# Retention, a mixture of experts and a dense layer on one core: float32 scores without splits, expert rows gathered tile by tile, gates applied to the dense result

## The chip, the core and the metric

The kernel runs on one core of a Trainium2 chip. The core has five engines that work from queues of their own: PE (TensorE, matrix products; PEld is its loading of the stationary operand), DVE (VectorE), ACT (ScalarE), POOL (GpSimd) and SP (SyncE, which here only starts DMAs). POOL also starts the indirect DMAs, which fetch or send rows by a list of row numbers. [...] The metric is the time of one execution on the device in microseconds (us): 1457.0 as the median of three runs (1452.89, 1457.00, 1457.19).

## The reference

Three stages follow each other, in float32 (the dense weights come as float64):

```python
# retention: B, H, S, D = 8, 8, 576, 64
scores = scale * np.matmul(q, k.transpose(0, 1, 3, 2))
ret = scores * np.where(rel >= 0, gamma[:, None, None] ** rel, 0.0)
x = np.matmul(ret, v)                                   # -> 4608 tokens of 512 features
# experts: 8 of them, 512 -> 1024 -> 512, the best one for each token
logits = x @ w_gate
expert_idx = np.argmax(logits, axis=1)
probs = softmax(logits)                                 # sum + 1e-09
gate_w = probs[np.arange(N), expert_idx]
out[mask] = gate_w[mask, None] * (np.maximum(x[mask] @ w1[e], 0.0) @ w2[e])
# dense: 512 -> 2048 -> 512
r = np.maximum(out @ w_in, 0.0)
result = (r * r) @ w_out
```

## The kernel before

The 4608 tokens are 36 tiles of 128. The order of the instructions on each engine is the order in which the code is written (a manual schedule); the framework puts in the semaphores. Pools with a fixed number of buffers decide when a transfer may start.

**Retention** (the loop `for t in range(NT)`, lines 592 to 635). SP loads one tile's q, k and v four tiles ahead (`load(t + 4)`, line 595) into a pool of five buffers. For each tile PE makes the scores of the next tile (`scores(t + 1)`, line 613), every second tile the router's logits (line 417), then the output `out_x(t)` (lines 385 and 389) and the running state `state(t)` (line 361). DVE multiplies the scores by a mask (line 343), scales the output (line 397) and transposes it (line 399); SP writes it to DRAM as `x_d`. ACT copies the state (line 368). POOL scales v (line 316). After some tiles DVE also does the routing of a group of tiles, one step for each turn of the loop.

Two ways to make the scores are in the code. The first `EASY = 2` tiles multiply k and q in plain float32: for each of four pairs of heads two products, one on partitions 0 to 63 and one on 64 to 127 (line 330). All later tiles first go through `split(t + 3)` (lines 293 to 312): k and q are rounded to float32r (ACT, lines 299 and 302), the remainders are taken (DVE and POOL, lines 303 and 306), and q is laid into `qb`, whose other half is zero, so that one product of 128 rows and 256 columns covers two heads. Three such products (high by high, high by low, low by high: lines 338 to 340) make one score.

**Experts** (lines 649 to 947). Work goes by units: `u = 8 * e + f` is one eighth of expert `e`. A unit's first product (`first`, lines 746 to 748) is made one unit ahead of its second (`second`, lines 770 to 772); both are split in float32r, three products each. Each expert has 640 slots for tokens, five tiles. `gather(e + 1)` fetches all five tiles at the start of expert `e`: 20 indirect DMAs on POOL, in one go, into a pool `xs_p` of one buffer. Five more fetch the logits of those tokens (`fetch_logits`, one unit later). `transp` transposes and splits one tile in each of the units `f = 2` to `6` (DVE line 718, ACT line 722, DVE line 723). `gate_of` makes the gates, and `finish` scales the result by them and sends the rows to `y_d`. At unit `REST = 18` a branch (line 793) skips the work for tokens beyond the slots; here it is skipped.

**Dense layer** (lines 950 to 1046): nine blocks of 512 tokens, two products (line 971, and lines 992 to 994), the square between them, and `store`, which copies the result out of PSUM.

Of the kernel before, what the change touches and what calls it, by code (L numbers as in the profile page):

```python
# [27 lines left out]
EASY = 2  # L28
BUSY = 6
# [10 lines left out]
def body(ctx, tc, att, tab_v, tab_x, masks, wg, ident, pick, cst, wu, wd, out):  # L40
# [19 lines left out]
    l_d = dram.tile([NTOK, NE], F32, name="l_d")  # L60
# [3 lines left out]
    cf = const.tile([128, C_N], F32, name="cf")  # L64
    ub = places.tile([128, 128], BF16, name="ub")
# [45 lines left out]
    # ---- float64 weights: sign, exponent and 20 bits of the mantissa come from the high word, the  # L111
    # other 32 bits from the low word; kept in DRAM as two float32r parts ----
# [99 lines left out]
    def fetch_logits(sm, index, n):  # L212
        lg = sm.tile([128, n, NE], F32, tag="lg", name="glg")
        for i in range(n):
            fetch_rows(lg[:, i], l_d[:, :], index[:, i:i + 1])
        return lg
# [18 lines left out]
    def gate_of(sm, lg, n):  # L235
        mx = sm.tile([128, n], F32, tag="mx", name="gmx")
        vec.tensor_reduce(out=mx, in_=lg, axis=AX.X, op=ALU.max)
        vec.tensor_tensor(out=lg, in0=lg, in1=mx.unsqueeze(2).to_broadcast([128, n, NE]), op=ALU.subtract)
        act.activation(out=lg, in_=lg, func=AF.Exp)
        vec.tensor_reduce(out=mx, in_=lg, axis=AX.X, op=ALU.add)  # L240
        vec.tensor_scalar(out=mx, in0=mx, scalar1=1e-9, scalar2=None, op0=ALU.add)
        g = sm.tile([128, n], F32, tag="g", name="gg")
        vec.reciprocal(out=g, in_=mx)
        return g
# [3 lines left out]
    # ================= retention, logits and routing =================  # L248
# [5 lines left out]
    with ExitStack() as es:  # L254
# [17 lines left out]
        qb = [[tabs.tile([128, 4, 2, 128], F32R, name=f"qb{i}{s}") for s in range(2)] for i in range(3)]  # L272

        in_t, vs_t, k_t, r_t, st_acc, xp_t = {}, {}, {}, {}, {}, {}
# [18 lines left out]
        def split(t):  # L293
            q = in_t[t][:, 0].rearrange("p (h n) -> p h n", h=4)
            k = in_t[t][:, 1]
            qh, ql = qb[t % 3]
            kh = sp_p.tile([128, 512], F32R, tag="kh", name="kh")
            kl = sp_p.tile([128, 512], F32R, tag="kl", name="kl")
            act.activation(out=kh, in_=k, func=AF.Copy)
            for s in range(2):  # L300
                o = slice(64 * s, 64 * s + 64)
                act.activation(out=qh[o, :, s], in_=q[o], func=AF.Copy)
            (pool if t > EASY else vec).tensor_tensor(out=kl, in0=k, in1=kh.bitcast(F32), op=ALU.subtract)
            for s in range(2):
                o = slice(64 * s, 64 * s + 64)
                (pool if s and t > BUSY else vec).tensor_tensor(
                    out=ql[o, :, s], in0=q[o], in1=qh[o, :, s].bitcast(F32), op=ALU.subtract
                )
            k_t[t] = kh, kl
# [12 lines left out]
        def scores(t):  # L322
            m = msk[:, 1 if kind(t)[1] == 4 else 0]
            sc = [sc_ps.tile([128, 4, 128], F32, tag="sc", name="sc") for _ in range(2)]
            for p in range(4):
                cs = slice(128 * p, 128 * p + 128)
                if t < EASY:
                    for s in range(2):
                        o = slice(64 * s, 64 * s + 64)
                        pe.matmul(  # L330
                            sc[s][:, p], in_t[t][o, 1, cs], in_t[t][o, 0, cs],
                            start=True, stop=True, skip_group_check=True,
                        )
                    continue
                qh, ql = [a[:, p].rearrange("p s n -> p (s n)") for a in qb[t % 3]]
                kh, kl = [a[:, cs] for a in k_t[t]]
                o = sc[p // 2][:, 2 * (p % 2):2 * (p % 2) + 2].rearrange("p s n -> p (s n)")
# [251 lines left out]
        if EASY < 3:  # L589
            split(2)  # L590
        fold = None
        for t in range(NT):
# [29 lines left out]
            if BUSY < t < NT - 3:  # L622
                split(t + 3)
# [501 lines left out]
```

## Time and profile before

| what | us |
|---|---|
| median of three runs | 1457.0 |
| span of the profiled execution, first to last instruction | 1541.4 |
| of it retention, to the last transpose of a tile | about 203 |
| of it experts | about 205 to 766 |
| of it the dense layer | about 766 to 1541 |

What lies around the span is not shown by the page. Over the whole span PE is busy 94%, DVE 50%, ACT 32%, POOL 26%; the 16 DMA engines moved 172.51 MB. These are means over three stages with different limits, so the rows below are taken stage by stage. [...] A table by lines gives instructions that share line, operation and shape: their busy time, the mean of one in ns, and the engine's idle time before them with what ended it.

### The profile page before, as it was taken

To read this page: it belongs to the slowest core of one execution; us is meant where nothing else is said; L and a number is where in the kernel's file an instruction comes from. 1 tells how busy PE (TensorE), PEld (TensorE's weight loads), DVE (VectorE), ACT (ScalarE), POOL (GpSimd) and SP (SyncE) were. 2 spreads that over 40 slices of the span, in tenths; PEclk is the share of its full clock that TensorE was granted. 3 is DMA by queue.
4 is the path that set the end of the run, shared out by engine and by line. 5 is a ranking of instruction groups with operands and counts; after the bars stand their busy time and mean duration, and the time that the engine had idled before them with its cause. 6 is when DMAs were issued, how large, how long until landed. Compare 5 with 4: busy or idle time off the path is not lost.

```text
span 1541.4 us, 20420 instructions
## 1 busy us (share of the span) xinstructions
PE 1445.4 (94%) x8081; PEld 1229.0 (80%) x8081; DVE 769.3 (50%) x1231; ACT 496.3 (32%) x866; POOL 397.0 (26%) x347
## 2 busy tenths in 40 slices
PE   7989899886979798789999999999999999999998
PEld 6878788685968687679888888888888888888887
DVE  7898965584848486574333333323232333323222
ACT  4555524242424243233222222222222222222222
POOL 5877736726354454711100000000000000000000
PEclk9999999988989899889999999999999999999999
DMA  8887634654546364634560202020200202020000
GB/s 308 277 265 251 206 115 141 217 166 150 187 142 218 117 223 144 197 110 183 162 252 5 51 0 55 1 55 1 55 1 1 55 1 55 1 55 0 28 0 28
DMA packets 92407, 172.51 MB, mean 112 GB/s; under 512 B 16654, under 2 KB 54030, under 8 KB 86672
## 3 DMA queue, kind: packets, MB, share of 16 engines
q1 hardware_dynamic: 82944, 151.03, 31.1%
q0 software_dynamic: 9360, 20.10, 4.1%
q8 instruction: 65, 1.06, 0.3%
q14 instruction: 38, 0.31, 0.1%
HBM read 125.86 MB, written 46.28 MB: 112 GB/s over the span
## 4 chain that ended last, share of the span: by engine, by line
PE 59%; issue 4%; DMA 1%; DVE 1%; POOL 0%; SPq 0%; ACT 0%; POOLq 0%; DVEq 0%
PE fl L971 25%; PE fa L994 8%; PE fa L993 8%; PE fa L992 8%; PE l L746 2%; PE l L747 2%; PE l L748 2%; PE acc L772 1%; PE acc L771 1%; PE acc L770 1%; DMA w<-wd_d 1%; DMA y_d<-y,sidx 0%; POOL y_d L229 0%; SPq L667 0%; DVE w L100 0%
## 5 line engine op out<-in xcount | busy, mean ns | idle before, releaser
L971 PE MATMUL fl<-xt,w 128*128 128x512 f32 (+1 forms) x1776 | 416.9, 384 | 1.8 <-DMA w<-wd_d 1.8
L971 PEld LDWEIGHTS fl<-xt,w 128*128 128x128 f32 x1776 | 328.1, 189 | 68.2 <-issue 2.2
L978 DVE TENSOR_TENSOR fr<-fr 128x512 f32<-128x512 f32 x144 | 99.9, 694 | 402.9 <-ACT fr L976 402.9
L992 PE MATMUL fa<-w,gh 128*128 128x512 f32 x576 | 224.1, 389 | 0.0
L993 PE MATMUL fa<-w,gh 128*128 128x512 f32 x576 | 224.1, 389 | 0.0
L994 PE MATMUL fa<-w,gl 128*128 128x512 f32 x576 | 224.1, 389 | 0.0
L976 ACT ACTIVATE fr<-fl 128x512 f32<-128x512 f32 x144 | 86.2, 599 | 417.6 <-PE fl L971 417.6
L746 PE MATMUL l<-xt,w 128*128 128x320 f32 (+1 forms) x480 | 154.9, 323 | 35.5 <-issue 17.5
L748 PE MATMUL l<-xt,w 128*128 128x320 f32 (+1 forms) x480 | 154.2, 321 | 11.0 <-issue 10.7
L747 PE MATMUL l<-xt,w 128*128 128x320 f32 (+1 forms) x480 | 154.5, 322 | 8.5 <-issue 8.4
L208 POOL DMA_INDIRECT xs<-x_d,qidx x140 | 151.0, 1078 | 44.3 <-issue 42.4
L982 DVE TENSOR_TENSOR gl<-fr,gh 128x512 fp32r<-128x512 f32 x144 | 99.7, 692 | 100.5 <-ACT gh L980 100.5
L772 PE MATMUL acc<-w,hl 128*128 128x512 f32 x320 | 127.4, 398 | 4.1 <-issue 3.7
L771 PE MATMUL acc<-w,hh 128*128 128x512 f32 x320 | 128.7, 402 | 2.3 <-issue 1.9
L770 PE MATMUL acc<-w,hh 128*128 128x512 f32 x320 | 128.9, 403 | 1.8 <-issue 1.8
L746 PEld LDWEIGHTS l<-xt,w 128*128 128x128 f32 x480 | 93.7, 195 | 45.3 <-issue 38.9
L980 ACT ACTIVATE gh<-fr 128x512 fp32r<-128x512 f32 x144 | 91.0, 632 | 109.8 <-DVE fr L978 109.8
L993 PEld LDWEIGHTS fa<-w,gh 128*128 128x128 f32 x576 | 108.2, 188 | 22.5
L992 PEld LDWEIGHTS fa<-w,gh 128*128 128x128 f32 x576 | 108.1, 188 | 22.5
L994 PEld LDWEIGHTS fa<-w,gl 128*128 128x128 f32 x576 | 108.0, 188 | 22.3
L753 DVE SCALAR_TENSOR_TENSOR hl<-l,hh 128x320 fp32r<-128x320 f32 (+2 forms) x128 | 59.9, 486 | 118.9 <-ACT hh L752 60.3
L747 PEld LDWEIGHTS l<-xt,w 128*128 128x128 f32 x480 | 94.0, 196 | 13.9 <-issue 11.4
(154 smaller groups left out, 1895.5 us busy)
## 6 DMA issues: line engine op xcount, KB each, us to landing
raw<-wu SPq DMA_DIRECT2D x62, 512.0 KB
in<-att SPq DMA_DIRECT2D x28, 1024.0 KB
craw<-wd SPq DMA_DIRECT2D x32, 512.0 KB
wd_d<-cw SPq DMA_DIRECT2D x32, 512.0 KB
w<-wd_d SPq DMA_DIRECT2D x16, 1024.0 KB
x_d<-xr SPq DMA_DIRECT2D x144, 64.0 KB
yi<-y_d SPq DMA_DIRECT2D x32, 256.0 KB
out<-fo SPq DMA_DIRECT2D x32, 256.0 KB
```

Source lines behind the costliest of these rows:

```text
L208: pool.indirect_dma_start(out=xs, out_offset=None, in_=src, in_offset=bass.IndirectOffsetOnAxis(ap=index, axis=0),)
L746: pe.matmul(ps, w[:, 0, k], hi[:, k, cs], start=(k == 0), stop=False)
L747: pe.matmul(ps, w[:, 0, k], lo[:, k, cs], start=False, stop=False)
L748: pe.matmul(ps, w[:, 1, k], hi[:, k, cs], start=False, stop=(k == 3))
L770: pe.matmul(acc[i], hh[:, cs], w[:, 0], start=(f == 0), stop=False)
L771: pe.matmul(acc[i], hh[:, cs], w[:, 1], start=False, stop=False)
L772: pe.matmul(acc[i], hl[:, cs], w[:, 0], start=False, stop=(f == 7))
L971: pe.matmul(ps, w[:, s, k], x[:, k, ts], start=(n == 0), stop=(n == 11))
L978: vec.tensor_tensor(out=gg, in0=r, in1=r, op=ALU.mult)
L992: pe.matmul(acc[i], gh[:, cs], w[:, 0], start=(f == 0), stop=False)
L993: pe.matmul(acc[i], gh[:, cs], w[:, 1], start=False, stop=False)
L994: pe.matmul(acc[i], gl[:, cs], w[:, 0], start=False, stop=(f == 15))
```

## The change

It has three parts. The constants `EASY` and `BUSY` go, and with them the tile pools' `qb` and the function `split`.

1. All tiles make the scores in plain float32, as the first two did. What is left of `split` is `spread_q`, two ACT copies for every ninth tile, now written ahead of `out_x(t)`. The zeroing of `qb` on POOL goes. The four weight splits that fall into the retention loop move from DVE to POOL.
2. `gather(e, i)` fetches one tile. Expert 1's five tiles are fetched in the units 0 to 4; those of expert `e + 2` in the units `f = 3` to `7` of expert `e`, each right behind the transpose that frees its place. The gathered rows have one buffer for good.
3. The gates leave the experts. Since relu and the square follow, a gate g on a row of the dense layer's input is g squared on the row of its result. `gates` makes the squares of all tokens in one go from the logits in SBUF; `store` multiplies by them. The table of logits in DRAM, its writes, the 40 fetches and `gate_of` go.

```diff
-        def split(t):
-            ...
+        def spread_q(t):
             if kind(t)[1] == 4:
+                q = in_t[t][:, 0].rearrange("p (h n) -> p h n", h=4)
                 act.activation(out=zq[:, :, 0], in_=q[:, :, 0:64], func=AF.Copy)
                 act.activation(out=zq[:, :, 2], in_=q[:, :, 64:128], func=AF.Copy)
...
         def scores(t):
             for p in range(4):
                 cs = slice(128 * p, 128 * p + 128)
-                if t < EASY:
-                    ...
-                pe.matmul(o, kh, qh, start=True, stop=False, skip_group_check=True)
-                pe.matmul(o, kh, ql, start=False, stop=False, skip_group_check=True)
-                pe.matmul(o, kl, qh, start=False, stop=True, skip_group_check=True)
+                for s in range(2):
+                    o = slice(64 * s, 64 * s + 64)
+                    pe.matmul(
+                        sc[s][:, p], in_t[t][o, 1, cs], in_t[t][o, 0, cs],
+                        start=True, stop=True, skip_group_check=True,
+                    )
...
-            if BUSY < t < NT - 3:
-                split(t + 3)
+            if t + 3 < NT:
+                spread_q(t + 3)
             out_x(t)
             state(t)
-            if t <= BUSY:
-                split(t + 3)
             if t % 6 == 2 and 12 <= t < 36:
-                w_q[t // 6 - 2] = split_unit(t // 6 - 2, raw.pop(t - 2), vec)
+                w_q[t // 6 - 2] = split_unit(t // 6 - 2, raw.pop(t - 2), pool)
...
+        def gates(lg):
+            e = rt.tile([128, NT, NE], F32, tag="ge", name="ge")
+            m = rt.tile([128, NT], F32, tag="gm", name="gm")
+            vec.tensor_reduce(out=m, in_=lg, axis=AX.X, op=ALU.max)
+            vec.tensor_tensor(out=e, in0=lg, in1=m.unsqueeze(2).to_broadcast([128, NT, NE]), op=ALU.subtract)
+            act.activation(out=e, in_=e, func=AF.Exp)
+            vec.tensor_reduce(out=m, in_=e, axis=AX.X, op=ALU.add)
+            vec.tensor_scalar(out=m, in0=m, scalar1=1e-9, scalar2=None, op0=ALU.add)
+            vec.reciprocal(out=m, in_=m)
+            vec.tensor_tensor(out=gate2, in0=m, in1=m, op=ALU.mult)
...
         first(4, (0,))
+        gates(lgt)
...
-            if e + 1 < NE:
-                if f == 0:
-                    gather(e + 1)
-                if f == 1:
-                    lg_t[e + 1] = fetch_logits(sm, gidx[:, CT * (e + 1):CT * (e + 2)], CT)
+            if u < CT:
+                gather(1, u)
             if e + 1 < NE and 2 <= f < 7:
                 transp(e + 1, f - 2)
+            if e + 2 < NE and f >= 3:
+                gather(e + 2, f - 3)
...
         def finish(e, tiles=range(CT)):
-                    vec.tensor_scalar(out=y, in0=acc[i], scalar1=g[:, i:i + 1], scalar2=None, op0=ALU.mult)
+                    vec.tensor_copy(y, acc[i])
...
         def store(b, tiles=range(4)):
-                    vec.tensor_copy(o, acc[i])
+                    vec.tensor_scalar(out=o, in0=acc[i], scalar1=g2, scalar2=None, op0=ALU.mult)
```

How the instructions stand now is seen best on PE, DVE and POOL. First PE in the retention loop, from the scores of tile 4 to the state of tile 3, before:

```order
L338 MATMUL sc<-qb_148,kh 128x256
L339 MATMUL sc<-qb_149,kh 128x256
L340 MATMUL sc<-qb_148,kl 128x256
...
L417 MATMUL lg<-x,wg_139 32x256 x4
L385 MATMUL x<-in,sts_142 128x128 x4
L389 MATMUL x<-r_362,vs 64x128 x4
L389 MATMUL x<-r_364,vs 64x128 x4
L361 MATMUL stp<-vs,in 64x64 x8
```

The same place of PE's queue in the changed kernel:

```order
L306 MATMUL sc<-in 128x128 x8
L386 MATMUL lg<-x,wg_139 32x256 x4
L354 MATMUL x<-in,sts_142 128x128 x4
L358 MATMUL x<-r_312,vs 64x128
L358 MATMUL x<-r_314,vs 64x128
...
L330 MATMUL stp<-vs,in 64x64 x8
```

Twelve products that read split copies (`qb`, `kh`, `kl`) have become eight that read the loaded tile `in`. DVE in one turn of the same loop, with a fold of the logits (`lgt`), before:

```order
L343 TENSOR_TENSOR r_624<-sc,msk 128x512
L343 TENSOR_TENSOR r_626<-sc,msk 128x512
L427 TENSOR_REDUCE lgt<-lg 128x16
L397 TENSOR_TENSOR x<-x,tabx 128x4x128
L399 STREAM_TRANSPOSE xr<-x 128x4x4x32
L306 TENSOR_TENSOR qb_147<-in,qb_146 64x4x128
```

The same turn on DVE now:

```order
L312 TENSOR_TENSOR r_526<-sc,msk 128x512
L312 TENSOR_TENSOR r_528<-sc,msk 128x512
L396 TENSOR_REDUCE lgt<-lg 128x16
L366 TENSOR_TENSOR x<-x,tabx 128x4x128
L368 STREAM_TRANSPOSE xr<-x 128x4x4x32
```

The remainder of q (`qb`) has gone, and nothing has taken its place. POOL from the end of the routing on, through expert 0 into expert 1 (`xs` are gathered rows, `glg` gathered logits, `w` a weight split, `y_d` the rows sent), before:

```order
L208 DMA xs<-x_d,gidx 128x512 x3
L108 TENSOR_TENSOR w<-half,w 128x512
L208 DMA glg<-l_d,gidx 128x8 x5
L208 DMA xs<-x_d,qidx 128x128 x20
L208 DMA glg<-l_d,gidx 128x8 x5
L100 TENSOR_TENSOR w<-raw,w 128x1024
L229 DMA y_d<-y,sidx 4608x512 x5
L208 DMA xs<-x_d,qidx 128x128 x20
```

The same stretch of POOL's queue now:

```order
L206 DMA xs<-x_d,gidx 128x512 x3
L106 TENSOR_TENSOR w<-half,w 128x512
L206 DMA xs<-x_d,qidx 128x128 x32
L98 TENSOR_TENSOR w<-raw,w 128x1024
L206 DMA xs<-x_d,qidx 128x128 x8
L221 DMA y_d<-y,sidx 4608x512 x5
L206 DMA xs<-x_d,qidx 128x128 x12
L98 TENSOR_TENSOR w<-raw,w 128x1024
```

The fetches of logits are gone. The 32 fetches that now stand in one row are those of expert 1 and the first three tiles of expert 2, interleaved: 16 for expert 1's tiles 0 to 3, four for expert 2's tile 0, four for expert 1's tile 4, eight for expert 2's tiles 1 and 2.

## Rows read from the trace of the kernel before

**Rows 1.** Stretches: us; PE, PEld, DVE, ACT, POOL busy (instructions); clock; DMA share; GB/s.

```profile
8.90:10.20 1.30, 1.27 (x20) 1.15 (x22) 0.00 (x0) 0.00 (x0) 0.00 (x0) 1.00 1.00 356
20.00:200.00 180.00, 160.74 (x1916) 141.79 (x1915) 163.23 (x265) 94.90 (x189) 128.79 (x96) 0.95 0.79 246
...
766.00:1541.00 775.00, 769.60 (x3387) 636.40 (x3386) 247.52 (x363) 201.36 (x330) 0.00 (x0) 1.00 0.13 37
10.00:20.00 10.00, 6.53 (x56) 5.95 (x56) 7.23 (x9) 4.31 (x8) 5.00 (x4) 0.73 1.05 414
60.00:180.00 120.00, 104.56 (x1258) 92.60 (x1255) 111.85 (x183) 64.16 (x127) 93.28 (x69) 0.94 0.83 261
...
203.00:226.00 23.00, 22.56 (x164) 19.79 (x163) 12.89 (x42) 7.54 (x16) 9.02 (x9) 1.00 0.47 139
```

**Rows 2.** Lines by shape, 20 to 200 us: busy us, mean ns, idle before.

```profile
L306 POOL TENSOR_TENSOR qb<-in,qb 64x512 fp32r<-64x512 f32 x29 | 45.2, 1557 | 3.0 <-PE turn L224 0.8
L343 DVE TENSOR_TENSOR r<-sc,msk 128x512 f32<-128x512 f32 x68 | 43.2, 675 | 0.1
L303 POOL TENSOR_TENSOR kl<-in,kh 128x512 fp32r<-128x512 f32 x32 | 43.0, 1345 | 32.4 <-ACT kh L299 32.4
...
L306 DVE TENSOR_TENSOR qb<-in,qb 64x512 fp32r<-64x512 f32 x36 | 39.6, 1101 | 12.2 <-ACT qb L302 12.1
...
L100 DVE TENSOR_TENSOR w<-raw,w 128x1024 fp32r<-128x1024 f32 x4 | 5.9, 1478 | 0.0
...
L451 DVE TENSOR_TENSOR eq<-lgt,mx 128x64 f32<-128x64 f32 x3 | 2.6, 860 | 0.1
```

**Rows 3.** Timeline, tile 1: start us, us, instruction; plain scores, then tile 0's output.

```profile
8.93 1.16 PE L330 MATMUL sc<-in 64*128 64x128 f32 x16 [2.64 <-DMA in<-att]
...
10.02 1.09 PE L389 MATMUL x<-r,vs 128*64 128x128 f32 x16
```

**Rows 4.** Timeline: first and last split scores of one tile; tile 22, load to scores.

```profile
104.09 0.60 SPq L291 DMA_DIRECT2D in<-att  x1
...
104.80 0.39 PE L338 MATMUL sc<-qb,kh 128*128 128x256 f32 x1
...
106.20 0.28 PE L340 MATMUL sc<-qb,kl 128*128 128x256 f32 x1
...
111.68 0.63 ACT L299 ACTIVATE kh<-in 128x512 fp32r<-128x512 f32 x1 [0.85 <-DMA in<-att]
...
118.29 0.39 PE L338 MATMUL sc<-qb,kh 128*128 128x256 f32 x1
```

**Rows 5.** Waits, 20 to 200 us: us in total, times, longest.

```profile
ACT kh L299 <- DMA in<-att: 30.6, 17, 3.5
```

**Rows 6.** Users of the loaded tile: ns min/median/max, first to last start us.

```profile
L299 ACT ACTIVATE kh<-in x34: 622/631/633, 12.0 to 181.7; 128x512 fp32r<-128x512 f32 x34
...
L306 DVE TENSOR_TENSOR qb<-in,qb x39: 642/1331/1579, 13.3 to 184.3; 64x512 fp32r<-64x512 f32 x39
```

**Rows 7.** Stretches in the experts; columns as in rows 1.

```profile
279.00:673.00 394.00, 331.86 (x1676) 287.71 (x1676) 248.35 (x403) 134.06 (x229) 196.02 (x179) 0.90 0.52 167
385.00:420.00 35.00, 35.00 (x199) 31.95 (x198) 29.47 (x51) 16.67 (x30) 9.39 (x8) 1.00 0.56 184
```

**Rows 8.** Waits of PE, 279 to 673 us; the first of several such rows.

```profile
PE l L746 <- issue: 17.3, 18, 1.9
```

**Rows 9.** Timelines by engine: gathering for expert 1, its last tile, PE's first unit.

```profile
226.57 1.89 POOL L208 DMA_INDIRECT xs<-x_d,qidx  x1 [1.91 <-DVE qidx L729]
...
254.56 0.95 POOL L208 DMA_INDIRECT xs<-x_d,qidx  x1 [0.31 <-issue]
...
258.63 0.71 DVE L718 STREAM_TRANSPOSE xf<-xs 128x512 f32<-128x512 f32 x1 [2.38 <-DMA xs<-x_d,qidx]
260.04 0.69 DVE L723 TENSOR_TENSOR xt<-xf,xt 128x512 fp32r<-128x512 f32 x1 [0.70 <-ACT xt L722]
...
261.99 0.31 PE L746 MATMUL l<-xt,w 128*128 128x320 f32 x1
```

More of the change, by code (lines that the diff above doesn't have):

```diff
@@ L64, in body @@
     cf = const.tile([128, C_N], F32, name="cf")
+    gate2 = const.tile([128, NT], F32, name="gate2")
     ub = places.tile([128, 128], BF16, name="ub")
@@ L210, in fetch_rows @@
         )
[L212 to L216, printed above, removed]
     x_q = x_d.rearrange("n (a c) -> (n a) c", a=4)
@@ L271, in body @@
         sts = [tabs.tile([128, 4, 128], F32, name=f"sts{i}") for i in range(4)]
-        qb = [[tabs.tile([128, 4, 2, 128], F32R, name=f"qb{i}{s}") for s in range(2)] for i in range(3)]
-        in_t, vs_t, k_t, r_t, st_acc, xp_t = {}, {}, {}, {}, {}, {}
+        in_t, vs_t, r_t, st_acc, xp_t = {}, {}, {}, {}, {}
         lead_s = []
@@ L291, in load @@
                 sp.dma_start(out=a[:, 0:n], in_=att[t, :, 0:n])
-        def split(t):
[L294 to L309, printed above, removed]
+        def spread_q(t):
             if kind(t)[1] == 4:
+                q = in_t[t][:, 0].rearrange("p (h n) -> p h n", h=4)
                 act.activation(out=zq[:, :, 0], in_=q[:, :, 0:64], func=AF.Copy)
@@ L442, in one @@
                 lg = lgt[:, t0:t1]
-                late.append(
-                    lambda: sp.dma_start(
-                        out=l_d[128 * t0:128 * t1, :].rearrange("(t p) e -> p t e", p=128), in_=lg
-                    )
-                )
                 mx = rt.tile([128, n], F32, tag="mx", name="mx")
@@ L581, in body @@
         vec.memset(wg2, 0.0)
-        for i in (0, 1, 2):
-            for a in qb[i]:
-                pool.memset(a[0:64, :, 1].bitcast(F32), 0.0)
-                pool.memset(a[64:128, :, 0].bitcast(F32), 0.0)
         scale_v(0)
@@ L588, in body @@
         scale_v(1)
-        if EASY < 3:
-            split(2)
         fold = None
@@ L695, in body, with gather @@
         acc_a = scope(es, "acc_a", 1, PSUM, reuse="tile")
-        xs_t, xt_t, lg_t, h_t, acc, gate = {}, {}, {}, {}, {}, {}
-        def gather(e):
-            xt_t[e] = columns()
-            xs = xs_p.tile([128, CT, 4, 128], F32, tag="xs", name="xs")
-            for i in range(0 if e else LEAD, CT):
-                j = CT * e + i
-                if e == 0:
-                    fetch_rows(xs[:, i].rearrange("p q c -> p (q c)"), x_d[:, :], gidx[:, j:j + 1])
-                    continue
-                for q in range(4):
-                    fetch_rows(xs[:, i, q], x_q, qidx[:, q, j:j + 1])
-            xs_t[e] = xs
+        xt_t, h_t, acc = {}, {}, {}
+        xs = xs_p.tile([128, CT, 4, 128], F32, tag="xs", name="xs")
+        def gather(e, i):
+            j = CT * e + i
+            if e == 0:
+                fetch_rows(xs[:, i].rearrange("p q c -> p (q c)"), x_d[:, :], gidx[:, j:j + 1])
+                return
+            for q in range(4):
+                fetch_rows(xs[:, i, q], x_q, qidx[:, q, j:j + 1])
         def transp(e, i):
-            xs = xs_t[e]
+            if e not in xt_t:
+                xt_t[e] = columns()
             hi, lo = [a[:, :, 128 * i:128 * i + 128] for a in xt_t[e]]
@@ L774, in finish @@
         def finish(e, tiles=range(CT)):
-            g = gate[e]
             for i in tiles:
@@ L861, in body @@
         indices(rt, NS, inv, gidx, sidx, gidf)
-        gather(0)
+        for i in range(LEAD, CT):
+            gather(0, i)
         for f in ends:
@@ L882, in body @@
         y_p = scope(es, "y_p", 5, reuse="tile")
-        sm = scope(es, "sm", 2, reuse="tile")
         lp = scope(es, "lp", 1, reuse="tile")
@@ L894, in body @@
         second(5, tiles)
-        lg_t[0] = fetch_logits(sm, gidx[:, 0:CT], CT)
         first(0, (1,))
```

40 lines of the change are left out of this document (8 added, 32 removed).

## The prediction

> **What bounds the kernel now.** I read the stretches first, then lines, waits and timelines inside the stretch that matters.
>
> The dense layer is PE alone: 769.6 of 775 us busy at a granted clock of 1.00 [rows 1]. Nothing that the change does there is on PE.
>
> In the experts PE also sets the pace, where nothing disturbs it: 199 products in 35.0 us [rows 7]. At that pace the 1676 products from 279 to 673 us would take 1676 / 199 x 35.0 = 294.8 us. They took 394: 99.2 us are lost. PE stands there without a semaphore to wait for ("issue") [rows 8], and its mean clock was 0.90 [rows 7]. Now the profiled span is 1541.4 us and the median of the timed runs 1457.0, 84.4 less, and neither of the other two stages shows a loss of that size. So I take it that the timed runs hold at most 99.2 - 84.4 = 14.8 us of it, less if some time lies around the span. [...] So every term below is taken off the median; the span of a profiled execution of the new kernel may differ from its timed runs by another amount.
>
> Retention is where several limits stand close together. From 20 to 200 us there are 34 tiles (two rows of line 343 each), 5.29 us a tile [rows 1, 2]. DVE is busy 163.2 of 180 us, PE 160.7, POOL 128.8, the DMA engines 0.79. No engine is full, and yet ACT waits 30.6 us for loads [rows 5]. The reason is a ring. Tile 22's load is issued at 104.09, its data are there at 111.68 (7.6 us), and its scores start at 118.29, after 6.6 us of splitting on ACT, DVE and POOL [rows 4]. Then the tile keeps its buffer through its scores, its output one turn later and its state: some two turns. With five buffers a turn P must satisfy 5 P >= 7.6 + 6.6 + 2 P, so P >= 4.7 us, before any jitter. That and DVE's 4.8 us a tile (163.2 / 34) make the 5.29.
>
> **The change, part by part.**
>
> PE's scores. Twelve split products start every (106.20 - 104.80) / 11 = 0.127 us, 1.53 us a tile [rows 4]. Eight plain ones (16 records, since each is recorded twice) run from 8.93 to the next product at 10.02: 1.09 us, at a clock of 1.00 [rows 1, 3]. The pairs on the two halves of the partitions overlap in this. So PE saves 0.44 us a tile, 15 us in 34 tiles, and its 160.7 us become 145.7, 4.29 a tile.
>
> [...] In the row the output of the other shape starts at 10.02, before the modelled end of the scores at 10.09 [rows 3], so no gap is seen. [...]
>
> DVE, POOL, ACT. DVE loses 39.6 us of remainders and the four weight splits, 5.9 us [rows 2]: 163.2 - 45.5 = 117.7, 3.46 a tile. It stops being a limit. POOL loses 45.2 + 43.0 = 88.2 us and gains four splits; one is twice as large as a remainder of 1.345 us [rows 2], so an estimate of 2.7 each, 11 in all. POOL goes from 128.8 to some 52 us. DVE's remainders took 642 ns at best and 1579 at worst [rows 6], so DVE is held up while POOL works; less of that remains, and I count it as nothing, because DVE now has a third of its time to spare. ACT loses all roundings. Its two copies for every ninth tile now stand ahead of the state's copies and wait for a load that was issued two turns before; at 7.6 us a load against two turns of 4.6 that costs nothing, and 3 us four times if it comes late.
>
> The ring. Without the 6.6 us it needs 5 P >= 7.6 + 2 P, P >= 2.5. It is no limit any more, and SP can issue a load as soon as a state is done.
>
> What is late next. PE needs 145.7 us for the 34 tiles, the DMA engines 0.79 x 180 = 142 us at a share of 1. The best case is that PE waits for nothing: 180 - 146 = 34 us gained. The worst is that PE keeps all of its present idle time, 19.3 us: 15 us gained. I take 24, a stretch of 156 us, nearer to the middle since the wait that the ring made goes and the one for the DMA engines comes: they would be busy 142 / 156 = 0.91. That can be had: 1.05 stands from 10 to 20 us, at 414 GB/s, with loads in large pieces [rows 1]. A share of 0.83 over two thirds of the stage, at a pace that the ring held back, is the row against more.
>
> The tail. The last tile's data are there at 181.7 us [rows 6]. Its 6.6 us of splitting lie behind that. Between 0 and 6.6 us go; I take half, 3.
>
> The gates. Six operations on DVE and one on ACT come in between routing and experts, none longer, by its row, than the 0.86 us of a similar subtraction [rows 2]: 0 to 5.2 us on DVE. Queued behind them are the transposed rows and the remainders for expert 0. PE is busy 22.56 of 23 us there [rows 1], so a delay of DVE can show; but DVE itself is busy 12.89 of 23. I take 1.5. What goes for it (fetches of logits, the gates of each expert) lay beside PE's work, and the multiplies in `finish` and `store` are passes over the same data on the same engines with or without a gate; PE covers them all but the last one. Together nothing.
>
> The gathers. POOL took from 226.57 to 255.51 for 20 fetches, 1.45 us each [rows 9]. It starts when the row numbers are there, so it can start no sooner. Expert 1's last tile was fetches 17 to 20 and is now 21 to 24, because four for expert 2 are written ahead: 4 x 1.45 = 5.8 us later. Before, its transpose began at 258.63 and its remainder was done at 260.73; PE's second half of the first unit, which reads it, began at 261.99, so there were 1.3 us to spare. Now PE waits 5.8 - 1.3 = 4.5 us, and behind the waiting transpose on DVE stand the remainder of the unit before and a weight split. It can be 0, if the fetches go faster, and 8, if the clock falls during the wait. I take +4.5. From expert 2 on each tile is fetched five units or more ahead, so those waits go; of the 14.8 us that the timed runs may have lost in the experts I count none in the forecast.
>
> Sum: 1457.0 - 24 - 3 + 1.5 + 4.5 = 1436.0 us. The forecast's own range is 1424 (retention 34) to 1448 (retention 15 and the higher costs).
>
> **The rivals.**
>
> A. The DMA engines are the limit already. If they get no better share than the 0.83 of the middle of the stage [rows 1], the stretch takes 142 / 0.83 = 171 us, 9 gained, no tail gained, and the gates and gathers eat most: 1457 - 9 + 6 = 1454. For it: the share is near 1 where loads run undisturbed. Against it: loads waited for buffers, not buffers for loads.
>
> B. The loss in the experts is in the timed runs after all. It came while POOL issued 25 fetches in a row; spread over units of 7 us they leave room. Then up to 14.8 us more go: 1421. Were the profile longer for a reason that the trace does not show, it could be the whole 99 us, 1337. For it: the loss repeats with the fetches. Against it: the 84.4 us.
>
> C. Slower than before: the clock. TensorE's clock was granted at 0.73 from 10 to 20 us, where PE was busy 65%, and at 0.95 where it was busy 89% [rows 1]. [...] Each tile has 4.29 us of PE work at full speed and as much again at half. The net gain of 21 us is gone when one seventh of the tiles (21 / (34 x 4.29) = 0.14) run at the lower level beyond today's share; at half of them the time is 1436 + 73 = 1509. Against it: by the sum PE is busier than before, 93% of 156 us, and the two plain tiles ran at 1.00.
>
> **How the numbers follow.** Forecast 0.67, A 0.12, B 0.15 (0.03 of it for the far end), C 0.06. The time is the forecast's, 1436. The range, 1416 to 1450, holds the forecast but for its upper edge, the near end of B and a part of A. About 0.3% (4.4 us) is what a measurement of this kernel can tell from no change, so "same" is 1452.6 to 1461.4: most of A, a little of the forecast and of C, 0.10. Faster: 0.65 + 0.15 + 0.05 = 0.85. Slower: 0.05, nearly all C.
>
> **What would show it.** Right, if the profile after has retention some 25 us shorter, DVE busy about two thirds of it, the DMA share near 0.9, and loads that land well before their scores. The scores' step is wrong if the 16 records of a tile take over 1.4 us; the ring's if loads still land just before they are used; the gathers' if the transpose of expert 1's last tile keeps its distance to PE. If the experts' loss without a semaphore is gone from the profile and the timed time falls by far more than 27 us, B holds. The forecast as a whole is wrong if the clock's mean in retention falls below 0.85.

## The result, and the profile after

The changed kernel takes 1435.5 us (median of four runs, 1433.25 to 1439.69), the kernel before 1455.6 us in the same comparison: a ratio of 0.988, 95% interval 0.9858 to 0.9902, some 20 us less. The forecast was 1436.0. So the number was met almost exactly, but the runs below show that three of the steps behind it were false and one was missing; their errors nearly cancelled, and that is luck. (A ratio in this document is taken without the runs that lie over 1.5% above the fastest of their kernel, while a median is that of all runs, so the two can differ a little.)

The span of the profiled execution is 1431.5 us, and its own time 1433.25: 1.75 us lie around the span. The stretches of the page's table, for the kernel after (us; PE, PEld, DVE, ACT, POOL busy and instructions; the clock granted to TensorE as a share of full speed; busy share of the DMA engines; GB/s), which answer to [rows 1] and the second to [rows 7]:

```profile
10.00:20.00 10.00, 8.61 (x142) 7.81 (x138) 6.35 (x10) 1.51 (x4) 3.13 (x3) 1.00 1.04 410
20.00:170.00 150.00, 133.12 (x1948) 114.72 (x1948) 104.03 (x214) 36.09 (x89) 45.19 (x38) 0.97 0.90 293
60.00:160.00 100.00, 89.97 (x1319) 77.66 (x1315) 72.20 (x152) 22.69 (x55) 32.32 (x27) 0.95 0.93 299
...
279.00:673.00 394.00, 388.83 (x2167) 352.49 (x2166) 274.27 (x429) 157.13 (x269) 148.69 (x131) 0.99 0.63 211
```

```profile
20.00:170.00 150.00, 132.56 (x1575) 116.84 (x1575) 135.80 (x210) 80.32 (x159) 109.90 (x83) 0.95 0.83 263
60.00:160.00 100.00, 84.82 (x1028) 74.97 (x1025) 92.27 (x144) 54.65 (x108) 78.45 (x59) 0.96 0.84 263
```

Three things stand in them. In retention DVE is busy 0.69 of the time where it was 0.91, and the DMA engines 0.90 and 0.93 in the two stretches from 20 and from 60 us, where the kernel before (second fence) has 0.83 and 0.84. In the experts (and the first part of the dense layer) PE makes 2167 products in the 394 us that held 1676 before: the stalls of [rows 7, 8] are not in this profile. And PE starts a tile's 16 plain score records at 64.81 and the next product at 65.90, 1.09 us, as in [rows 3]; behind that stand the logits, the output and the state of one turn (timeline, PE). As in [rows 3] the next product starts before the modelled end of the scores (65.90 against 64.81 + 1.16 = 65.97), so no gap of PE shows between the two shapes:

```profile
64.81 1.16 PE L306 MATMUL sc<-in 64*128 64x128 f32 x16
65.90 0.64 PE L386 MATMUL lg<-x,wg 128*32 128x256 f32 x8
66.47 1.09 PE L358 MATMUL x<-r,vs 128*64 128x128 f32 x16
67.40 0.63 PE L330 MATMUL stp<-vs,in 128*64 128x64 f32 x16
```

The lines of POOL and DVE between 20 and 175 us answer to [rows 2]: one weight split took 2.476 us on POOL, an estimate of 2.7 had stood for it, and the mask's multiply takes 678 ns, about the 675 of before, although POOL has far less to do.

```profile
L312 DVE TENSOR_TENSOR r<-sc,msk 128x512 f32<-128x512 f32 x64 | 40.8, 678 | 1.5 <-PE sc L306 0.9
L98 POOL TENSOR_TENSOR w<-raw,w 128x1024 fp32r<-128x1024 f32 x4 | 9.9, 2476 | 14.5 <-ACT w L97 10.9 <-DMA x_d<-xr 3.5
```

Retention ends (last transpose of a tile) at 175.3 us, against 203.3 in the profile of the kernel before. The waits of that stretch:

```profile
ACT sts L337 <- PE stp L330: 70.2, 26, 5.6
POOL vs L293 <- DMA in<-att: 53.7, 17, 5.2
...
ACT zq L288 <- DMA in<-att: 24.4, 4, 9.0
...
PE x L354 <- ACT sts L337: 10.6, 4, 4.4
...
PE sc L306 <- DMA in<-att: 4.4, 5, 1.7
```

PE's scores wait for loads only 4.4 us in all, but POOL waits for one 17 times, so loads still land just before they are used; the prediction had named that as the sign that its ring is wrong. And the two copies of every ninth tile (`spread_q`) come too late. ACT waits for that tile's load, the copies of the state are queued behind, and PE's output waits for those, here with 4.38 us (timeline, ACT and PE):

```profile
77.95 0.42 ACT L288 ACTIVATE zq<-in 128x256 f32<-128x256 f32 x1 [9.04 <-DMA in<-att]
79.52 2.07 PE L354 MATMUL x<-in,sts 128*128 128x128 f32 x8 [4.38 <-ACT sts L337]
```

This load was issued at 70.14 us, 7.8 us ahead of the copies and hardly slower than the 7.6 of the prediction; but it is written one turn ahead of the copies, not two (`load(t + 4)` stands in the turn ahead of the one whose `spread_q(t + 3)` reads the same tile). It happens at each of the four tiles and costs PE 10.6 us of the 16.9 that it is idle between 20 and 170 us.

One stage behaves as the prediction had not said: from its first product to the end the dense layer took 791.9 us before and 796.7 now.

**Why chips are named below.** The runs went to several chips, and on two of them (4 and 10) the kernel before takes 1542 and 1567 us, on another (8) 1451. So a kernel is compared with the kernel before on its own chip only, and stages with kernels on the same chip where there are any. Each chip was seen in one session only, so what is put down to a chip could also belong to the time of its session. The runs on record for the two kernels name no chip.

### The profile page after: what moved, and what is told of

Read it like the earlier page. It is cut to its first block, busy times and chain, and to the rows that moved or that the text cites. A ratio compares the mean times of both kernels' runs of the same rounds, so it can differ in the third digit from the quotient of the medians.

```text
span 1431.5 us, 20262 instructions
## 1 busy us (share of the span) xinstructions
PE 1395.7 (98%) x8217; PEld 1190.7 (83%) x8217; DVE 705.1 (49%) x1153; ACT 433.9 (30%) x757; POOL 264.4 (18%) x237
## 4 chain that ended last, share of the span: by engine, by line
PE 72%; issue 3%; DMA 1%; POOL 0%; SPq 0%; ACT 0%; DVE 0%; POOLq 0%
PE fl L920 27%; PE fa L942 9%; PE fa L943 9%; PE fa L941 9%; PE l L701 3%; PE l L703 3%; PE l L702 3%; PE acc L725 3%; PE acc L726 3%; PE acc L727 3%; DMA w<-wd_d 1%; DMA y_d<-y,sidx 0%; POOL y_d L221 0%; SPq L623 0%; DMA yi<-y_d 0%
## 5 line engine op out<-in xcount | busy, mean ns | idle before, releaser
L206 POOL DMA_INDIRECT xs<-x_d,qidx x140 | 148.1, 1058 | 109.5 <-DVE xf L673 62.9
L701 PE MATMUL l<-xt,w 128*128 128x320 f32 (+1 forms) x480 | 150.4, 313 | 7.7 <-DVEq L747 4.1
L702 PE MATMUL l<-xt,w 128*128 128x320 f32 (+1 forms) x480 | 150.1, 313 | 0.0
L703 PE MATMUL l<-xt,w 128*128 128x320 f32 (+1 forms) x480 | 150.1, 313 | 0.0
L725 PE MATMUL acc<-w,hh 128*128 128x512 f32 x320 | 125.6, 392 | 0.0
L726 PE MATMUL acc<-w,hh 128*128 128x512 f32 x320 | 125.3, 392 | 0.0
L701 PEld LDWEIGHTS l<-xt,w 128*128 128x128 f32 x480 | 91.0, 190 | 11.1 <-issue 4.5
L702 PEld LDWEIGHTS l<-xt,w 128*128 128x128 f32 x480 | 91.0, 190 | 2.3 <-DVE xt L678 0.2
L703 PEld LDWEIGHTS l<-xt,w 128*128 128x128 f32 x480 | 91.0, 189 | 0.0
```

What stands on the lines that cost most here:

```text
L206: pool.indirect_dma_start(out=xs, out_offset=None, in_=src, in_offset=bass.IndirectOffsetOnAxis(ap=index, axis=0),)
L701: pe.matmul(ps, w[:, 0, k], hi[:, k, cs], start=(k == 0), stop=False)
L702: pe.matmul(ps, w[:, 0, k], lo[:, k, cs], start=False, stop=False)
L703: pe.matmul(ps, w[:, 1, k], hi[:, k, cs], start=False, stop=(k == 3))
L725: pe.matmul(acc[i], hh[:, cs], w[:, 0], start=(f == 0), stop=False)
L726: pe.matmul(acc[i], hh[:, cs], w[:, 1], start=False, stop=False)
```

## The experiments

### The dense layer: a tile among the constants moves everything by 160 bytes

In the changed kernel a product on the weights of `f = 0` to `3` starts every 0.230 to 0.238 us. So do up to nine products right behind such ones; nearly all others start every 0.2267 (of some 1030 slow starts, 810 are on these weights). These four weights lie in `w_d`, which is laid out from the right end of SBUF; all else in the dense layer is laid out from the left, and `gate2`, 144 bytes among the constants, moves that by 160 bytes. (Before, these tiles and `w_d` begin at addresses that leave the same rest modulo 2048: 98272 for the transposed rows, 176096 for the squares, 196576 for `w_d`.) By surplus I mean the sum, over the 3504 products of the layer, of what each start lies more than 0.2268 us after the one ahead, where a distance counts as 0.3 us at most, so that a single long wait doesn't enter: 7.56 us after, 1.32 before.

First the changed kernel with a wider tile, then the kernel before with an unused one:

```diff
-    gate2 = const.tile([128, NT], F32, name="gate2")
+    gate2 = const.tile([128, 48], F32, name="gate2")[:, 0:NT]
```

> The changed kernel with one edit: the tile of the squared gates is 48 columns wide instead of 36, so that every tile that is laid out from the left lies 192 bytes above its place in the kernel before, not 160. In the changed kernel's trace the dense layer's products that read the weights of f = 0 to 3 (tile w_d, laid out from the right, not moved) start every 0.230 to 0.238 us instead of 0.2267; over the layer that is 7.6 us above 3504 x 0.2267, against 1.3 us in the kernel before. Placement theory: it is the shift of the left tiles against w_d by 160 bytes, an odd multiple of 32; with 192, a multiple of 64, these products are back at 0.2267, the dense layer's surplus falls below 2.5 us, and the time falls by 5 to 7 us, to about 1429. Rival (it is what the gates' move does to the dense layer, or its data): the products stay slow, the surplus stays near 7.6 us and the time near 1435.

```diff
     cf = const.tile([128, C_N], F32, name="cf")
+    pad = const.tile([128, NT], F32, name="pad")
```

> The kernel before with one edit: an unused tile of 36 columns among the constants, which moves all tiles that are laid out from the left up by 160 bytes; nothing else changes. Placement theory: products with the weights of f = 0 to 3 slow down to 0.230 to 0.238 us, the dense layer's surplus over 0.2267 us a product rises from 1.3 to about 7.6 us, and the time rises by 5 to 7 us (1.004 of the kernel before). Rival (gates or data): no change, within 1 us. The recorded stalls in the experts (99 us in the profile of before) are expected to be in this profile's span again, and not in its time.

The surplus was 6.55 us with 192 bytes, so a multiple of 64 doesn't help and that form of the theory fell. But it was 7.55 in the kernel before with an unused tile, so its cause is the place alone: no gate, no other data, no other instruction came in. (The times of the two, 1448.5 and 1545.1 beside 1542.2 for the kernel before, are from chip 4, whose stalls hide 6 us: the ratio of `b_pad160` is 1.0026, 0.998 to 1.0072.) The same twelve products, one weight tile against four token tiles, in `b_pad160` and below in the kernel before (timelines of PE; the first column is the start):

```profile
913.12 0.40 PE L993 MATMUL fa<-w,gh 128*128 128x512 f32 x1
913.36 0.39 PE L994 MATMUL fa<-w,gh 128*128 128x512 f32 x1
913.59 0.40 PE L995 MATMUL fa<-w,gl 128*128 128x512 f32 x1
...
915.92 0.39 PE L972 MATMUL fl<-xt,w 128*128 128x512 f32 x1
```

```profile
936.16 0.39 PE L992 MATMUL fa<-w,gh 128*128 128x512 f32 x1
936.39 0.39 PE L993 MATMUL fa<-w,gh 128*128 128x512 f32 x1
936.62 0.39 PE L994 MATMUL fa<-w,gl 128*128 128x512 f32 x1
...
938.88 0.39 PE L971 MATMUL fl<-xt,w 128*128 128x512 f32 x1
```

Twelve take 2.80 us in the one and 2.72 in the other, at a granted clock of 1.00 in both, and PE waits for no one. Then a shift that keeps every place modulo 2048 bytes:

```diff
-    gate2 = const.tile([128, NT], F32, name="gate2")
+    gate2 = const.tile([128, 512], F32, name="gate2")[:, 0:NT]
```

> The changed kernel with the tile of the squared gates 512 columns wide, so that the tiles laid out from the left lie 2048 bytes above their place in the kernel before. With 160 the dense layer's surplus over 0.2267 us a product was 7.56 us in the changed kernel, and 7.55 in the kernel before with an unused tile; with 192 it was 6.55; with 0 it is 0.7 to 1.3. In the kernel before all tiles, w_d among them, begin at the same place modulo 2048 bytes (98272, 176096, 196576 all leave 2016). Placement theory, alignment modulo a power of two up to 2048: the surplus falls below 2 us and the time is 5 to 7 us below the changed kernel on the same chip. Rival (any shift costs): it stays at 6 to 8 us.

The surplus is 0.65 us, the dense layer 789.7 us against 795.8 in the changed kernel on the same chip (`a_again`), and the time 1431.26 against 1435.48 (ranges that overlap, so the stage tells more than the time). The placement theory holds:

```profile
822.80 0.39 PE L941 MATMUL fa<-w,gh 128*128 128x512 f32 x1
823.03 0.39 PE L942 MATMUL fa<-w,gh 128*128 128x512 f32 x1
823.26 0.39 PE L943 MATMUL fa<-w,gl 128*128 128x512 f32 x1
...
825.52 0.61 PE L920 MATMUL fl<-xt,w 128*128 128x512 f32 x2
```

Over all profiles: shift 0, five profiles, 0.63 to 0.67 (1.32 in the one ahead of the prediction); 160, five profiles, 7.51 to 7.56; 192, one, 6.55; 2048, two, 0.64 and 0.65. The step of the prediction that was wrong is its shortest one, "nothing that the change does there is on PE".

### The stalls in the experts, part 2 and part 3 alone

From the 84.4 us between the profile's span and the median the prediction took it that the timed runs hold at most 14.8 us of PE's lost 99.2, an estimate from these numbers alone. The kernel before, profiled once more:

> The kernel before as it is, for a second profile. Theory that the stalls belong to some chips: if this chip's timed runs of the kernel before are near 1451 to 1457, its profile's span is 2 us below its own time, with retention about 196 us, experts 460 to 465 with less than 15 us of gaps in PE, and the dense layer 790; if the timed runs are near 1540, the experts take 530 to 550. Rival (the prediction's: the recording of a profile brings the stalls, the timed runs are without them): a span of 1520 us or more beside timed runs below 1460.

On chip 10 its span was 1562.7 us, the time of that same execution 1564.5, and 19 timed runs beside it took 1554 to 1589 us, with a median of 1567.4. So a profile's span is not longer than its own timed run, and the stalls are in the timed runs of such a chip. The prediction's premise is false: the profile that it read, whose own time isn't on record, is by its span of 1541.4 us (and some 1.8 around it, as in every execution here that has both) an execution of the kind that chip 4 gives (1524 to 1560), and the median of 1457 is of the kind that chip 8 gives (1444 to 1457). PE waits there for nothing that the profile shows, as in [rows 8] (waits, 254 to 700 us):

```profile
PE l L747 <- issue: 19.0, 20, 1.8
PE l L748 <- issue: 13.2, 16, 2.5
PE l L746 <- issue: 11.4, 17, 1.2
```

Not all of the 99.2 us is of this kind. In the profile ahead of the prediction 15.0 us are one single wait of PE at the branch (line 793; waits of PE, 279 to 673 us), and `b_gates` has one of 13.6; no other profile has more than 1.7 under this name. What holds the branch was not settled.

```profile
PE l L746 <- PEq L793: 15.0, 1, 15.0
```

Whether the recording has a part in the stalls stays open, since every timed run here comes with a span and a clock, and so is recorded too in some form.

Where the stalls come can be seen on chip 4. The kernel before fetches 25 times and sends 5 times in one row in every expert; the changed one has rows of 12 and 13. Between 350 and 560 us, first `b_pad160`, then `a_pad192`, same chip:

```profile
350.00:560.00 210.00, 173.08 (x863) 150.10 (x862) 130.04 (x212) 71.20 (x122) 90.08 (x81) 0.87 0.46 150
```

```profile
350.00:560.00 210.00, 210.00 (x1179) 191.73 (x1179) 167.05 (x262) 92.56 (x159) 111.96 (x100) 1.00 0.64 211
```

PE is never idle with short rows, and with long ones makes 863 products instead of 1179, the clock at 0.87. In `a_pad192` the one long row left, 40 fetches from 202 to 258 us with one weight split among them, stalls too, from about 30 us into it:

```profile
230.00:262.00 32.00, 16.87 (x55) 12.21 (x56) 8.99 (x15) 5.06 (x9) 22.33 (x22) 0.70 0.32 103
262.00:290.00 28.00, 28.00 (x156) 25.46 (x156) 20.16 (x31) 12.47 (x22) 10.34 (x10) 0.98 0.67 221
```

Parts 2 and 3 alone, on the same chip: in `b_spread` `gather(e, i)` as in the change, with the fetches of logits kept; in `b_gates` the change's `gates` and `store`, with `gather(e + 1)` at `f = 0` kept.

```diff
             if e + 1 < NE:
-                if f == 0:
-                    gather(e + 1)
                 if f == 1:
                     lg_t[e + 1] = fetch_logits(sm, gidx[:, CT * (e + 1):CT * (e + 2)], CT)
+            if u < CT:
+                gather(1, u)
             if e + 1 < NE and 2 <= f < 7:
                 transp(e + 1, f - 2)
+            if e + 2 < NE and f >= 3:
+                gather(e + 2, f - 3)
```

> The kernel before with the second part of the change alone: rows gathered one tile per unit, logits still fetched five in a row. The prediction priced this part at +4.5 us for expert 1's last tile and at 0 for the rest, with up to 14.8 us of gain if the stalls with the bursts of 25 fetches are in the timed runs (rival B). The trace of the changed kernel suggests a smaller cost: PE waits 2.0 us where expert 1's last tile comes late. Expected: +1 to +3 us, no more than 2 us of gain. If rival B holds: 5 to 15 us faster. In the profile the stalls of PE without a semaphore should be mostly gone, since the bursts are.

```diff
+        gates(lgt)
...
-                if f == 1:
-                    lg_t[e + 1] = fetch_logits(sm, gidx[:, CT * (e + 1):CT * (e + 2)], CT)
...
-            if f == 5:
-                gate[e] = gate_of(sm, lg_t.pop(e), CT)
```

> The kernel before with the third part of the change alone: the squares of the gates are made once and applied to the dense result. It brings in the tile of 144 bytes that moves the left tiles by 160. The prediction priced it at +1.5 us. Placement theory: +5 to +8 us, the dense layer's surplus near 7.6 us, the rest of the cost 1 us or less around the making of the gates. Without that theory: 0 to +2 us.

Against 1542.2 for the kernel before, `b_spread` took 1484.1 (ratio 0.966, 0.9601 to 0.9718) and `b_gates` 1497.1 (0.9753, 0.9695 to 0.981). Neither expectation had a gain of that size. PE's gaps (products in the experts that start over 0.42 us after the one ahead, less the usual distance) add up to some 70 us in `b_pad160`, 40 in `b_spread` and 36 in `b_gates`, where rows have 25 with the sends, not 30. Counted product by product, `b_spread` loses its time where it still has a long row, 28 fetches from 235 to 270 us: the first 500 of the 2508 products of the experts take 128.4 us, and 92.2 in `a_late2048` (chip 8, no stalls); the other 2008 take 366.5 and 364.4, with rows of 12 and 18. So the stalls go with long rows; which property of a row sets them off (its length, its pace or what else moves then) these runs don't separate. The dense layer's surplus in `b_gates` is 7.56, so its gain is a net of that loss. Rival B held on this chip: by the ratios the two gain some 52 and 38 us, where it had allowed at most 14.8 (or, as a far end, 99).

To see what fetches cost on a chip without stalls, the kernel before with a quarter of them:

```diff
-                for q in range(4):
-                    fetch_rows(xs[:, i, q], x_q, qidx[:, q, j:j + 1])
+                fetch_rows(xs[:, i].rearrange("p q c -> p (q c)"), x_d[:, :], gidx[:, j:j + 1])
```

> The kernel before, with one fetch of a whole row of 2 KB for each tile instead of four of 512 bytes: the same bytes with a quarter of the fetches, 10 in a row instead of 25 (the rows' features then stand in another order than the products expect, so the result is not the reference's; the work of all engines is otherwise unchanged). Theory that fetches in a row stall all engines: the 70 to 99 us of stalls go, the time on a chip with stalls falls from 1540 to 1450 to 1465 us; on a chip without them it stays within 3 us of the kernel before. Rival (the stalls are not the fetches'): within 1% of the kernel before on either.

It came to chip 8, which shows no stalls (the kernel before 1451.2), so it can't tell whether they would go. It took 1442.5, a ratio of 0.9938 (0.9919 to 0.9956): 8.7 us less, where within 3 was expected. So also there the kernel before loses some 9 us to its fetches, and it may be that part of that went with the change. Where these 9 us lie in the trace was not settled; the kernel before has no profile from chip 8.

### The order of the gathers

The changed kernel once more, and with the fetches for expert `e + 2` four units later:

> The changed kernel as it is, once more, so that the runs of this call have it beside them on the same chip. If this chip shows the stalls of the experts in its timed runs (the kernel before near 1540 us, as in the runs with b_pad160): 1445 to 1460 us, with some 20 us of PE's time lost while the first 40 to 57 fetches stand in one row, and a ratio near 0.94. If it does not (the kernel before near 1456): 1433 to 1440 and a ratio near 0.988. The dense layer's surplus is near 7.6 us in either case.

```diff
-            if e + 2 < NE and f >= 3:
-                gather(e + 2, f - 3)
+            n, i = divmod(u - 7, 8)
+            if n >= 0 and n + 2 < NE and i < CT:
+                gather(n + 2, i)
```

> As a_pad2048, and the rows of expert e + 2 are fetched three units ahead of their transposes (at the units 7, 0, 1, 2, 3 instead of 3 to 7), so that expert 1's last tile is not behind expert 2's first and the first row of fetches has 20, not 40 to 57. Theory that the stalls come with more than some 22 fetches in one row: the 20 us that a chip with stalls loses at 234 to 260 us in the changed kernel go, 10 to 25 us below a_pad2048 there, and 2 us below it on a chip without stalls (the wait for expert 1's last tile). Rival (stalls come with the rows' bytes or with the other transfers at that time, not with the row of fetches): no difference beyond 2 us.

All three ran on chip 8 beside 1451.2 for the kernel before. `a_again` took 1435.5 (0.9898, 0.9868 to 0.9929), `a_pad2048` 1431.3 (0.9861, 0.9817 to 0.9905), `a_late2048` 1425.5 (0.9838, 0.9791 to 0.9886): the best of all, 10 us below the changed kernel, of which 4 are the shift's and 6 the order's, where 2 were expected for the order. From the first product of the experts to that of the dense layer `a_late2048` took 456.8 us, and 461.9, 459.3 and 461.3 the three profiles with the change's order (`a_pad2048`, `a_again` and the changed kernel itself, whose chip isn't known): 2.5 to 5.1 us. Nearer to the spot, the first 400 products of that stage take 74.2 us, and 79.9, 79.8 and 78.0: the late tile costs 4 to 6 us there. 200 to 300 us in both (the stretches don't begin at the same product), `a_pad2048` first:

```profile
200.00:300.00 100.00, 96.48 (x523) 87.31 (x523) 67.29 (x104) 40.19 (x68) 71.96 (x63) 0.98 0.56 191
```

```profile
200.00:300.00 100.00, 100.00 (x557) 91.32 (x556) 74.19 (x115) 44.43 (x74) 62.92 (x57) 1.00 0.63 213
```

How the wait comes about stands in the trace of the changed kernel (timeline, DVE and PE; answers to [rows 9]). DVE waits 7.09 us for expert 1's last tile, the remainder `hl` of the unit before is queued behind it, and PE waits for that:

```profile
232.99 0.71 DVE L673 STREAM_TRANSPOSE xf<-xs 128x512 f32<-128x512 f32 x1 [7.09 <-DMA xs<-x_d,qidx]
234.40 0.69 DVE L678 TENSOR_TENSOR xt<-xf,xt 128x512 fp32r<-128x512 f32 x1 [0.69 <-ACT xt L677]
235.01 0.88 DVE L708 SCALAR_TENSOR_TENSOR hl<-l,hh 128x256 fp32r<-128x256 f32 x2
```

```profile
235.48 0.42 PE L701 MATMUL l<-xt,w 128*128 128x320 f32 x1 [1.68 <-DVE hl L708]
```

No chip with stalls ran `a_late2048`, so what it does there is not known.

### Retention: part 1 alone, and the ring

Part 1 alone in the kernel before (plain `scores` for every tile, `spread_q`, `split` and `qb` gone, the four weight splits on POOL):

> The kernel before with the first part of the change alone: plain scores, no splits, weight splits on POOL in the retention loop. The prediction priced it at -27 us (24 for the pace of the tiles, 3 for the tail), between -15 and -40.6; its rival A (the DMA engines are the limit already) at -9. Retention ends at 196.4 us in four profiles of kernels with split scores and at 170 to 179 in five with plain ones, so -18 to -26 us is expected, a retention of 170 to 179 us, and nothing in the experts and the dense layer (790 us).

On chip 10 it took 1549.9 us against 1567.4 (0.9912, 0.9861 to 0.9964). Its retention ends at 186.8 us, that of `b_again` on the same chip at 201.0: 14.2 us. On chip 4 split scores end at 198.2 us in three profiles and plain ones at 178.5; on chip 8 the figures are 198.1, and 180.4, 178.6 and 172.3 for the same code three times. So part 1 brings 14 to 26 us, about 20 in the middle, and one profile of it is worth no more than 4 us either way; 18 to 26 had been expected. PE's waits for the two copies of every ninth tile are in `b_plain` too, 15.2 us by the same rows, and 10.0 to 12.5 in the five profiles of the change with five buffers; in that of the kernel before they are 0.2.

Six buffers for the tiles in the kernel before, and three in the changed one:

```diff
-        in_p = scope(es, "in_p", 5)
+        in_p = scope(es, "in_p", 6)
```

> The kernel before with six buffers for the loaded tiles instead of five (the load is still written four tiles ahead, so it no longer waits for the tile just finished). Ring theory of the prediction: six turns must cover 7.6 + 6.6 us and two turns, a turn of 3.6 us, so the ring is no limit, DVE's 4.8 us a tile becomes it, and retention is 8 to 17 us shorter. Rival (the engines' own work, or the DMA engines, set the pace): within 3 us.

```diff
-        in_p = scope(es, "in_p", 5)
+        in_p = scope(es, "in_p", 3)
```

> The changed kernel with three buffers for the loaded tiles instead of five. Ring theory: 3 P >= 7.6 + 2 P, a turn of 7.6 us instead of 4.7, retention some 100 us longer (loads that land sooner with fewer in flight would bring it down to 5 to 6 us a turn, 20 to 40 us longer). Rival (buffers are held for less than two turns, or are not what loads wait for): within 10 us.

With six nothing moved: 1.0023 (0.9976 to 1.007), retention to 201.7 us against 201.0. The ring of the prediction is false. What would have told is a view that it did not use, the waits of SP's queue in the kernel before (20 to 170 us), where loads (L291) wait 8 us in all and SP stands 34.6 us at the writes of `x_d`, behind which the next load is written:

```profile
SPq L406 <- DVE xr L399: 34.6, 13, 5.7
...
SPq L291 <- PE stp L361: 2.6, 3, 2.3
```

With three buffers, in one profile, retention ends at 224.3 us, 6.06 us a tile, against 4.94 with five in `b_plain` on the same chip (4.6 to 4.8 elsewhere), and the load (L283) does wait for the state that frees its buffer (20 to 170 us):

```profile
SPq L283 <- PE stp L330: 66.7, 19, 8.8
```

So the formula describes a ring where buffers are few (3 x 6.06 less two turns leaves 6.06 us for the load, so not the 7.6 that it assumed), but five were not few. That the load's place in the program, four tiles ahead and behind the writes, sets the old pace would fit (about three turns for 7.6 + 6.6 us are 4.7 us each); a load written five tiles ahead was not tried, and the limit of the old loop stays open. What the runs show is that it goes with the splits.

## Why the prediction was right, and where it wasn't

The sum on chip 8, where the kernel before and the changed one differ by 1451.2 - 1435.5 = 15.7 us: retention -17.7 by one profile of each kind (198.1 to 180.4), the dense layer +6.1 (789.7 to 795.8), so -4 is left for the experts. The prediction had -27, 0 and +6. So 9 us of its gain did not come, 6 us of loss were left out, and 10 us of loss that it had counted were not there. On this chip 15.7 us are gained where 21 were forecast; that the comparison on record, with its 20 us, came so near was luck.

- **The scores, DVE, POOL:** as worked out. 1.09 us a tile, DVE at 0.69 of the time ("about two thirds"), 2.476 us for a split on POOL. How far POOL held DVE up is less plain: of the 39 remainders on DVE in the trace of before, the three beside an idle POOL took 0.67 to 0.69 us and all 25 of 0.86 us and more had POOL busy beside them, but so had 11 that took 0.64 to 0.72 us.
- **The ring:** false, as the run with six buffers shows. The 24 + 3 us that hung on it were too many: 14 to 26 us came. That is inside the bounds that the prediction set by PE's idle time (15 to 34) but for chip 10's 14.2.
- **The copies for every ninth tile:** put at nothing, because their load was taken to be two turns old, "and 3 us four times if it comes late". It came late four times out of four: 10.6 us of PE's waits. What the time would get back with the copies written a turn later was not tried, and the DMA engines at 0.90 to 0.93 (1.04 from 10 to 20 us) leave, by estimate, little room.
- **What is late next:** right. The DMA share was forecast at 0.91 and is 0.90 to 0.93; rival A, a share that stays at 0.83, is out.
- **The gates:** 1.5 us forecast. PE's products, counted one by one in the two profiles, lose 0.7 us between routing and experts; in `b_gates`, the gates alone, 0.1 by the same count.
- **The gathers:** right in mechanism and size, 4.5 us forecast and 4 to 6 measured in the first 400 products. The order of PE's loss was another than said: not at the tile's own products, but by the remainder queued behind its transpose.
- **The dense layer:** the missing term, +6.1 us, put at nothing with "nothing that the change does there is on PE". It can't be seen in any row of before, only in the addresses.
- **The stalls:** the premise that timed runs don't hold them is false on two of the chips seen. The chip that gave the result shows none in the changed kernel, in spite of 57 indirect DMAs nearly in one row (52 fetches and 5 sends), and a median of before below 1460, so taking the terms off 1457 was sound for it. Of the 14.8 us that the prediction left as a bound, up to 8.7 exist on such a chip; the forecast counted none. This term and the dense layer's are of about the same size and opposite.
- **The clock (rival C):** out; it is 0.95 to 0.97 in retention. The half speed that the rival reckons with is in the trace of the kernel before: 0.50 from 15 to 20 us, where split products start every 0.21 us, against 0.12 us from 105.02 to 106.20 us, at 1.00.

On a chip with stalls the same change is worth far more: `a_pad192`, the changed kernel but for a shift by 32 bytes, was at 0.9423 (0.9375 to 0.9471) on chip 4. The gain there is some 90 us where 21 were forecast.

## What to carry to other kernels

A gap between a profile's span and the timed median is first a question of which chip each came from: compare a profile with the time of its own execution before calling a loss the recording's. Read the waits of the queue that issues the loads before blaming the number of buffers. When work that waits for a load is written ahead of other work in an engine's queue, count in the trace how old the load is by then. And after a change to what lies in SBUF, look at the pace of products that the change doesn't touch.

## What the runs showed of the hardware

- In the dense layer a product whose operands lie in tiles 160 bytes off their common place modulo 2048 starts 1 to 5% later than one whose tiles agree (0.230 to 0.238 us against 0.2267 for 512 columns, in the changed kernel). The layer's surplus was 7.51 to 7.56 us with 160 bytes and 6.55 with 192, against 0.63 to 1.32 with none; with 2048 it was 0.64 and 0.65. It takes one operand in the moved part and one in the part that stayed: products with both in the moved part keep 0.2267, but for up to nine right behind slow ones. Which shifts between 192 and 2048 are free was not tried.
- With long rows of indirect DMAs on POOL (30 in 40 to 43 us in the trace of the kernel before) PE stalls on two of the three chips named here: 863 products in 210 us on chip 4 (`b_pad160`), where short rows let it make 1179 (`a_pad192`), and 43.6 us of waits without a semaphore at three lines on chip 10 (`b_again`). On the third, chip 8, the changed kernel with 57 nearly in one row doesn't (1435.5 us). The kernel before takes 1451 us on chip 8 and 1567 on chip 10.
